# A priority for the activation chain of the first 24 units in a Fourier-and-feed-forward kernel

## The chip, the cores and the metric

The kernel runs on one core of a Trainium2 chip. The metric is device time in microseconds (us) for one execution of the whole program; the time before is 1764.74 us, the median of three runs.

## The reference, cut to what matters

```python
X = np.fft.fft(x, axis=1)            # x: (8, 3008, 256) float32
X = np.fft.fft(X, axis=2)
x = X.real.astype(np.float32).reshape(8 * 3008, 256)
h = x @ w_in                         # w_in: (256, 2048) float64
g = np.where(h >= 1, h, np.where(h <= -1, 0.0, (h + 1) ** 2 / 4))
out = (g @ w_out).astype(np.float32) # w_out: (2048, 256) float64
```

The inputs `w_in` and `w_out` are 64-bit floats that were drawn in numpy, so the kernel receives 64-bit words and has to make 32-bit floats of them.

## The kernel before, in words

The eight batches are worked off one after the other. Each has 3008 rows, which the kernel holds as three chunks of 482 to 512 columns (`NCHUNK`, `WIDTH`). The column direction is 2048 hidden features in 16 tiles of 128 (`NFT`). A **unit** is one chunk by one feature tile; each batch has 48 units (`per`), the whole kernel 384.

A unit has three parts. `gemm1` (L359) makes two products `uv` on TensorE in six matmuls; the weights `wh`/`wl` and the data `pqh`/`pql` are each split into a high and a low part. Then comes the **activation**, nine instructions on three engines: VectorE makes `us` (L362) and the two signs of `h` (L364, L365), ScalarE a ReLU and a square (L372, L373), VectorE the min/max (L374), ScalarE the rounded copy `gh` (L375), GpSimd the remainder `gl` in two halves (L378). Last, `gemm2` (L402) adds 12 matmuls with `woh`/`wol` into four accumulators. `gemm2` of a unit is given out `LAG` = 4 units after its `gemm1`. The buffers `uv` number 3, `us` 2, `h` and `a` 3, `gh` and `gl` 4.

The first batch is different. Its 48 units go in two visits: units 0 to 23 take feature tiles 0 to 7 of all three chunks, units 24 to 47 take tiles 8 to 15 and add to what the first visit stored. Meanwhile the weights are still being made. They come in 16 jobs of 512 columns; `convert_w(n)` (in short c0 to c15) turns a job's 64-bit words into 32-bit floats in six or seven VectorE instructions and one or two ScalarE ones (for c6 to c15: L208, L217, L218, L221, L222, L223, L224, L225). Jobs of `w_out` are then split into `woh`/`wol` (`split_w_out`, L169 on ScalarE and L170 on VectorE); jobs of `w_in` go through a small matmul and are split into `wh`/`wl` (`fold_w_in`, `fold_delta`). The `STEPS` table says in front of which unit each of these is given out:

```python
    0: "o2", 1: "f1 d1 o3 p11", 2: "p12", 3: "p13 p14 l8 l9", 4: "c6",
    5: "o6 c7", 6: "o7 l10", 9: "c8", 11: "c9 l11", 13: "f2 d2 c10 l12",
    15: "c11 l13", 17: "o10 c12 l14", 18: "o11", 19: "c13 l15", 20: "c14",
    21: "f3 d3", 22: "c15", 25: "o14", 26: "o15",
```

(`p11` to `p14` are the last pieces of the Fourier transform of batch 0, which also end in a split by L169 and L170.) Job 6 is what `gemm2` of feature tiles 4 and 5 needs (first in unit 4), job 7 tiles 6 and 7; jobs 8 and 9 are needed by `gemm1` of unit 24, jobs 12 and 13 by that of unit 28, jobs 14 and 15 by `gemm2` of units 28 and 30.

The order on each engine is written by the language's scheduler when the program is built. Each instruction gets a place number in the order in which the code gives it out; at each moment an engine takes, of the instructions whose inputs and buffers are ready by the scheduler's reckoning, the one with the lowest place. `tc.high_priority(offset=n)` lowers the place numbers inside it by n and puts the counter back when it ends. After that the order on an engine is fixed. The code already uses it for the copies out of the accumulators (`EVICT_AHEAD`).

Of the kernel before, what the change touches and what calls it, by code (L numbers as in the profile page):

```python
# [1 line left out]

# [1 line left out]

# [23 lines left out]
NFT = FF // P  # L28
LAG = 4
EVICT_AHEAD = 150  # L30

C_ORDER = [*range(1, 8), 0, *range(8, NC)]
WIDTH = [7 * NA + 34, CH, CH]
# [76 lines left out]
def fft_ffn_kernel(ctx: ExitStack, tc: tile.TileContext, x, cst, w_in, w_out, out):  # L110
# [223 lines left out]
    units = []  # L334
# [7 lines left out]
    per = NCHUNK * NFT  # L342
    n_units = len(units)
    acts, outs = {}, {}
# [5 lines left out]
    def gemm1(i):  # L350
        b, k, f, *_ = units[i]
        n = WIDTH[k]
        hi, lo = pq[b, k]
        cols = slice(f * P, (f + 1) * P)
        uv = []
        for m in range(2):
            t = ps.tile([P, CH], F32, tag="uv", name=f"uv_{i}_{m}", bufs=3)
            for j, (w, r) in enumerate(((wh, hi), (wl, hi), (wh, lo))):
                nc.tensor.matmul(t[:, :n], w[m][:, cols], r[:, m, :n], start=(j == 0), stop=(j == 2))  # L359
            uv.append(t[:, :n])  # L360
        us = sb.tile([P, CH], F32, tag="us", name=f"us_{i}", bufs=2)[:, :n]
        nc.vector.scalar_tensor_tensor(us, nyb[b, k][:, :n], delta[:, f : f + 1], uv[0], op0=ALU.mult, op1=ALU.add)  # L362
        h = sb.tile([P, 2, CH], F32, tag="h", name=f"h_{i}", bufs=3)[:, :, :n]
        nc.vector.tensor_tensor(h[:, 0], us, uv[1], op=ALU.subtract)  # L364
        nc.vector.tensor_tensor(h[:, 1], us, uv[1], op=ALU.add)  # L365
        a = sb.tile([P, 2, CH], F32, tag="a", name=f"a_{i}", bufs=3)[:, :, :n]
        gh = sb.tile([P, 2, CH], F32R, tag="gh", name=f"gh_{i}", bufs=4)[:, :, :n]
        gl = sb.tile([P, 2, CH], F32R, tag="gl", name=f"gl_{i}", bufs=4)[:, :, :n]


        for sl in (slice(0, 2),) if i < n_units - 1 else (slice(0, 1), slice(1, 2)):
            nc.scalar.activation(a[:, sl], h[:, sl], AF.Relu, bias=half, scale=0.5)  # L372
            nc.scalar.activation(a[:, sl], a[:, sl], AF.Square)  # L373
            nc.vector.scalar_tensor_tensor(h[:, sl], a[:, sl], 1.0, h[:, sl], op0=ALU.min, op1=ALU.max)  # L374
            nc.scalar.activation(gh[:, sl], h[:, sl], AF.Copy)  # L375
        for sg in range(2):
            eng = nc.vector if sg and i >= n_units - 3 else nc.gpsimd
            eng.tensor_tensor(gl[:, sg], h[:, sg], gh[:, sg].bitcast(F32), op=ALU.subtract)  # L378
        acts[i] = gh, gl

    accs = []
    def gemm2(i):
# [15 lines left out]
        for dh, sg in banks:  # L398
# [6 lines left out]
            if last:  # L405

                dst = o[dh][:, sg, :n]
                with tc.high_priority(offset=EVICT_AHEAD):
                    if v:
# [42 lines left out]
    for i in range(n_units + LAG):  # L452
        run_steps(STEPS.get(i, ""))
        if i < n_units:
            b, r = divmod(i, per)
# [11 lines left out]
            while pending and (change or not soon and done < total * (r + 1 - r0) / (per - r0)):  # L467
                change = False
                w, f = pending.pop(0)
# [61 lines left out]
```

## Time and profile before

| | |
|---|---|
| median of three runs | 1764.74 us (1764.58 to 1770.89) |
| profiled execution | 1765.38 us, of which the span from first to last instruction 1763.6 |
| busy in the span | TensorE 98%, VectorE 82%, ScalarE 76%, GpSimd 68% |
| granted TensorE clock, mean | 0.997 of full speed |

Times in the rows below are microseconds from the start of the span, durations in us unless a column says ns. PE is TensorE, PEld its weight loads, DVE VectorE, ACT ScalarE, POOL GpSimd, SP the engine that issues DMAs. A row of a timeline reads: start, duration, engine, line, operation, output and inputs with shapes, how many, and in brackets how long the engine sat idle before it and what ended that. L12 is line 12 of the kernel.

### The profile page before, as it was taken

To read this page: it belongs to the slowest core of one execution; us is meant where nothing else is said; L and a number is where in the kernel's file an instruction comes from. 1 tells how busy PE (TensorE), PEld (TensorE's weight loads), DVE (VectorE), ACT (ScalarE), POOL (GpSimd) and SP (SyncE) were. 2 spreads that over 40 slices of the span, in tenths; PEclk is the share of its full clock that TensorE was granted. 3 is DMA by queue.
4 is the path that set the end of the run, shared out by engine and by line. 5 is a ranking of instruction groups with operands and counts; after the bars stand their busy time and mean duration, and the time that the engine had idled before them with its cause. 6 is when DMAs were issued, how large, how long until landed. Compare 5 with 4: busy or idle time off the path is not lost.

```text
span 1763.6 us, 21942 instructions
## 1 busy us (share of the span) xinstructions
PE 1735.8 (98%) x7982; PEld 1420.5 (81%) x7982; DVE 1440.0 (82%) x1766; ACT 1346.3 (76%) x1580; POOL 1202.1 (68%) x838
## 2 busy tenths in 40 slices
PE   9988999999999999999999999999999999999998
PEld 6766888888888788888888888888888888888877
DVE  6999788888887888878888788878888788888887
ACT  5777877777777877777778877788778787777776
POOL 1545966776768766787667876677676766667775
PEclk9999999999999999999999999999999999999999
DMA  7013321010010100110001100011000000000000
GB/s 230 12 66 101 101 104 60 28 50 30 13 51 28 53 30 1 51 48 33 30 10 51 50 28 24 22 39 50 28 24 34 1 23 32 11 25 5 19 25 24
DMA packets 29963, 72.51 MB, mean 41 GB/s; under 512 B 2976, under 2 KB 8224, under 8 KB 29856
## 3 DMA queue, kind: packets, MB, share of 16 engines
q1 hardware_dynamic: 29568, 70.08, 12.1%
q8 instruction: 62, 1.02, 0.2%
q10 hardware_dynamic: 288, 1.05, 0.2%
q14 instruction: 45, 0.37, 0.1%
HBM read 43.31 MB, written 27.81 MB: 40 GB/s over the span
## 4 chain that ended last, share of the span: by engine, by line
PE 61%; ACT 10%; POOL 9%; issue 6%; DVE 5%; ACTq 0%; POOLq 0%; DVEq 0%
PE acc L402 38%; PE uv L359 19%; POOL gl L378 9%; DVE h L374 4%; ACT a L373 4%; ACT gh L375 3%; ACT a L372 3%; PE s L270 2%; PE s L309 2%; ACT z L280 1%; DVE o L414 0%; DVE h L365 0%; DVE h L364 0%; POOL y L131 0%; ACT o L412 0%
## 5 line engine op out<-in xcount | busy, mean ns | idle before, releaser
L378 POOL TENSOR_TENSOR gl<-h,gh 128x512 fp32r<-128x512 f32 (+1 forms) x765 | 1095.1, 1454 | 513.3 <-ACT gh L375 491.7
L374 DVE SCALAR_TENSOR_TENSOR h<-a,h 128x1024 f32<-128x1024 f32 (+1 forms) x385 | 578.0, 1502 | 219.7 <-ACT a L373 218.1
L375 ACT ACTIVATE gh<-h 128x1024 fp32r<-128x1024 f32 (+1 forms) x385 | 400.6, 1041 | 356.9 <-DVE h L374 344.2
L402 PE MATMUL acc<-gh,woh 128*128 128x512 f32 (+1 forms) x1536 | 608.3, 396 | 6.7 <-ACT gh L375 3.3
L402 PE MATMUL acc<-gl,woh 128*128 128x512 f32 (+1 forms) x1536 | 604.6, 394 | 9.1 <-POOL gl L378 9.1
L402 PE MATMUL acc<-gh,wol 128*128 128x512 f32 (+1 forms) x1536 | 596.2, 388 | 0.0
L372 ACT ACTIVATE a<-h,biases 128x1024 f32<-128x1024 f32 (+1 forms) x385 | 431.7, 1122 | 10.0 <-DVE h L365 7.7
L373 ACT ACTIVATE a<-a 128x1024 f32<-128x1024 f32 (+1 forms) x385 | 398.8, 1036 | 7.1
L402 PEld LDWEIGHTS acc<-gl,woh 128*128 128x128 f32 x1536 | 288.8, 188 | 76.4 <-POOL gl L378 16.8
L402 PEld LDWEIGHTS acc<-gh,woh 128*128 128x128 f32 x1536 | 289.3, 188 | 68.9 <-DVE o L414 5.5
L402 PEld LDWEIGHTS acc<-gh,wol 128*128 128x128 f32 x1536 | 289.5, 188 | 59.2
L364 DVE TENSOR_TENSOR h<-us,uv 128x512 f32<-128x512 f32 (+1 forms) x384 | 259.3, 675 | 67.2 <-POOL gl L378 27.3
L359 PE MATMUL uv<-pqh,wh 128*128 128x512 f32 (+1 forms) x768 | 303.7, 395 | 3.0 <-DVE us L362 2.9
L359 PE MATMUL uv<-pql,wh 128*128 128x512 f32 (+1 forms) x768 | 301.4, 392 | 0.0
L359 PE MATMUL uv<-pqh,wl 128*128 128x512 f32 (+1 forms) x768 | 299.5, 390 | 0.0
L362 DVE SCALAR_TENSOR_TENSOR us<-nyb,delta,uv 128x512 f32<-128x512 f32 (+1 forms) x384 | 278.5, 726 | 14.6 <-PE uv L359 13.8
L365 DVE TENSOR_TENSOR h<-us,uv 128x512 f32<-128x512 f32 (+1 forms) x384 | 256.0, 667 | 0.0
L359 PEld LDWEIGHTS uv<-pqh,wh 128*128 128x128 f32 x768 | 144.4, 188 | 40.9 <-DVE us L362 6.8
L359 PEld LDWEIGHTS uv<-pql,wh 128*128 128x128 f32 x768 | 144.6, 188 | 32.1
L359 PEld LDWEIGHTS uv<-pqh,wl 128*128 128x128 f32 x768 | 144.4, 188 | 30.5 <-issue 0.2
L131 POOL TENSOR_TENSOR y<-x 96x512 f32<-96x512 f32 x60 | 106.4, 1774 | 20.0 <-DMA x<-in_x_dram 8.2
L280 ACT ACTIVATE z<-s 64x192 f32<-64x192 f32 x256 | 86.6, 338 | 6.5 <-PE s L275 1.7
(54 smaller groups left out, 548.0 us busy)
## 6 DMA issues: line engine op xcount, KB each, us to landing
x<-in_x_dram SPq DMA_DIRECT2D x64, 384.0 KB, 3.3
out_dram<-o SPq DMA_DIRECT2D x30, 512.0 KB, 2.8
out_dram<-o SPq DMA_DIRECT2D x16, 482.0 KB, 3.0
nyb<-nyr SPq DMA_DIRECT2D x24, 256.0 KB, 3.4
raw<-in_moe_w_out_dram SPq DMA_DIRECT2D x8, 512.0 KB, 10.9
raw<-in_moe_w_in_dram SPq DMA_DIRECT2D x6, 512.0 KB, 4.5
part<-o SPq DMA_DIRECT2D x4, 512.0 KB, 3.2
o<-part SPq DMA_DIRECT2D x4, 512.0 KB
```

What stands on the lines that cost most here:

```text
L131: nc.gpsimd.tensor_tensor(y, t[:, 0], t[:, 1], op=ALU.add)
L280: nc.scalar.activation(dst, src, AF.Copy)
L359: nc.tensor.matmul(t[:, :n], w[m][:, cols], r[:, m, :n], start=(j == 0), stop=(j == 2))
L362: nc.vector.scalar_tensor_tensor(us, nyb[b, k][:, :n], delta[:, f : f + 1], uv[0], op0=ALU.mult, op1=ALU.add)
L364: nc.vector.tensor_tensor(h[:, 0], us, uv[1], op=ALU.subtract)
L365: nc.vector.tensor_tensor(h[:, 1], us, uv[1], op=ALU.add)
L372: nc.scalar.activation(a[:, sl], h[:, sl], AF.Relu, bias=half, scale=0.5)
L373: nc.scalar.activation(a[:, sl], a[:, sl], AF.Square)
L374: nc.vector.scalar_tensor_tensor(h[:, sl], a[:, sl], 1.0, h[:, sl], op0=ALU.min, op1=ALU.max)
L375: nc.scalar.activation(gh[:, sl], h[:, sl], AF.Copy)
L378: eng.tensor_tensor(gl[:, sg], h[:, sg], gh[:, sg].bitcast(F32), op=ALU.subtract)
L402: nc.tensor.matmul(acc[:, :n], w[:, f, wc], g[:, sg], start=(first and j == 0), stop=(last and j == 2))
```

## The change

The nine instructions of the activation move from `gemm1` into a function of their own, which `gemm1` calls at the same place. For units 0 to 23 (`per // 2` is 24) the call stands inside `tc.high_priority(offset=60)`; for all later units in an empty context. No instruction is added, removed or changed.

```diff
+AHEAD = 60
...
                 nc.tensor.matmul(t[:, :n], w[m][:, cols], r[:, m, :n], start=(j == 0), stop=(j == 2))
             uv.append(t[:, :n])
+
+        with tc.high_priority(offset=AHEAD) if i < per // 2 else nullcontext():
+            acts[i] = activate(i, uv)
+
+    def activate(i, uv):
+        b, k, f, *_ = units[i]
+        n = WIDTH[k]
         us = sb.tile([P, CH], F32, tag="us", name=f"us_{i}", bufs=2)[:, :n]
         nc.vector.scalar_tensor_tensor(us, nyb[b, k][:, :n], delta[:, f : f + 1], uv[0], op0=ALU.mult, op1=ALU.add)
...
             eng.tensor_tensor(gl[:, sg], h[:, sg], gh[:, sg].bitcast(F32), op=ALU.subtract)
-        acts[i] = gh, gl
+        return gh, gl
```

## Rows read from the trace of the kernel before

**Rows 1.** The page's first part: engines over the whole span.
```profile
PE 1735.8 (98%) x7982; PEld 1420.5 (81%) x7982; DVE 1440.0 (82%) x1766; ACT 1346.3 (76%) x1580; POOL 1202.1 (68%) x838
```

**Rows 2.** Busy time by stretch: window, its length, engines, granted clock, DMA.
```profile
37.00:170.00 133.00, 118.71 (x518) 89.81 (x517) 125.34 (x183) 96.89 (x115) 63.70 (x48) 0.99 0.17 54
170.00:260.00 90.00, 86.54 (x415) 70.69 (x414) 71.81 (x89) 70.96 (x97) 71.27 (x49) 1.00 0.31 98
260.00:500.00 240.00, 239.88 (x1125) 199.65 (x1124) 196.84 (x234) 185.66 (x216) 170.65 (x118) 1.00 0.12 39
```

**Rows 3.** TensorE's waits from 37 to 170: us in total, times, longest.
```profile
PE acc L402 <- POOL gl L378: 6.9, 13, 1.2
PE acc L402 <- ACT gh L375: 3.3, 3, 1.5
PE uv L359 <- DVE us L362: 2.9, 3, 1.3
PE s L309 <- DVE pql L170: 1.0, 1, 1.0
```

**Rows 4.** Timeline at 88 to 92.
```profile
88.21 0.42 DVE L217 TENSOR_SCALAR cv<-raw 128x512 uint32<-128x512 uint32 x1
88.54 0.42 DVE L221 TENSOR_SCALAR raw<-raw 128x512 uint32<-128x512 uint32 x1
88.88 0.68 DVE L218 SCALAR_TENSOR_TENSOR cv<-cv,cps 128x512 f32<-128x512 uint32 x1
...
90.61 0.74 DVE L362 SCALAR_TENSOR_TENSOR us<-nyb,delta,uv 128x512 f32<-128x512 f32 x1
...
91.41 0.50 PE L359 MATMUL uv<-pqh,wh 128*128 128x512 f32 x1 [1.35 <-DVE us L362]
```

**Rows 5.** VectorE's work by line, 37 to 170: busy us, mean ns, idle before.
```profile
L374 DVE SCALAR_TENSOR_TENSOR h<-a,h 128x1024 f32<-128x1024 f32 (+1 forms) x24 | 31.1, 1296 | 0.8 <-ACT a L373 0.5
L362 DVE SCALAR_TENSOR_TENSOR us<-nyb,delta,uv 128x512 f32<-128x512 f32 (+1 forms) x26 | 18.8, 727 | 5.0 <-PE uv L359 5.0
L364 DVE TENSOR_TENSOR h<-us,uv 128x512 f32<-128x512 f32 (+1 forms) x25 | 16.6, 666 | 0.0
L217 DVE TENSOR_SCALAR cv<-raw 128x512 uint32<-128x512 uint32 x10 | 7.3, 735 | 0.0
L224 DVE SCALAR_TENSOR_TENSOR cps<-raw,cps 128x512 uint32<-128x512 uint32 x10 | 6.9, 687 | 0.0
L223 DVE TENSOR_SCALAR cps<-raw 128x512 uint32<-128x512 f32 x10 | 6.8, 685 | 0.2 <-ACT raw L222 0.2
L225 DVE SCALAR_TENSOR_TENSOR cv<-cv,cps 128x512 f32<-128x512 f32 x10 | 6.8, 677 | 0.0
L218 DVE SCALAR_TENSOR_TENSOR cv<-cv,cps 128x512 f32<-128x512 uint32 x10 | 6.8, 676 | 0.0
L221 DVE TENSOR_SCALAR raw<-raw 128x512 uint32<-128x512 uint32 x10 | 5.3, 533 | 0.0
```

**Rows 6.** The same line L374 in the steady part, 260 to 1700.
```profile
L374 DVE SCALAR_TENSOR_TENSOR h<-a,h 128x1024 f32<-128x1024 f32 (+1 forms) x329 | 499.7, 1519 | 209.1 <-ACT a L373 207.9
```

**Rows 7.** TensorE's timeline at 130, and the stretch behind it.
```profile
130.28 0.50 PE L402 MATMUL acc<-gh,woh 128*128 128x512 f32 x1 [1.51 <-ACT gh L375]
132.00:135.00 3.00, 3.00 (x8) 2.35 (x8) 3.00 (x7) 2.22 (x3) 0.82 (x1) 0.50 0.85 287
```

**Rows 8.** Timeline: job 6 from its first VectorE step to its first use; job 7's last step and use.
```profile
51.53 0.42 DVE L217 TENSOR_SCALAR cv<-raw 128x512 uint32<-128x512 uint32 x1
62.76 0.69 DVE L170 TENSOR_TENSOR wol<-cv,woh 128x512 fp32r<-128x512 f32 x1
65.71 0.51 PE L402 MATMUL acc<-gh,woh 128*128 128x482 f32 x1
70.60 0.69 DVE L170 TENSOR_TENSOR wol<-cv,woh 128x512 fp32r<-128x512 f32 x1
78.35 0.38 PE L402 MATMUL acc<-gh,woh 128*128 128x482 f32 x1
```

**Rows 9.** Timeline of VectorE: the end of job 15's conversion.
```profile
162.67 0.68 DVE L225 SCALAR_TENSOR_TENSOR cv<-cv,cps 128x512 f32<-128x512 f32 x1
```

**Rows 10.** SP's waits over the whole span, as in rows 3; TensorE's waits from 165 to 260.
```profile
SPq L123 <- DVE cv L225: 9.6, 1, 9.6
SPq L189 <- DVE cv L225: 7.7, 1, 7.7
...
PE acc L402 <- POOL gl L378: 2.2, 3, 1.4
PE s L270 <- ACT z L280: 1.5, 2, 1.1
```

More of the change, by code (lines that the diff above doesn't have):

```diff
@@ L1 @@
-from contextlib import ExitStack
+from contextlib import ExitStack, nullcontext
 import numpy as np
```

## Prediction

> **What bounds the kernel now.** I read the page's engine shares first, then the busy time by stretch, then the waits and the work by line inside the stretch that the change touches. Over the whole span TensorE is busy 98% [rows 1], so the kernel can only get faster by the 2% in which it isn't. The stretches show where these are [rows 2]. From 260 to 500 us TensorE is idle for 240 − 239.88 = 0.1 us; there is nothing to win in the steady part. From 37 to 170 us, which is about where units 0 to 23 have their activations, it is idle for 133 − 118.71 = 14.3 us, and from 170 to 260 for 90 − 86.54 = 3.5 us. So the change plays for at most 14.3 us, or 0.8%, and a little that hangs on it.
>
> In the same stretch the other column to look at is VectorE: 125.34 of 133 us, 94%, against 71.81 of 90 right behind it and 82% later [rows 2]. It is VectorE that is full here, and TensorE's waits name it by its victims [rows 3]: 6.9 us for `gl`, 3.3 us for `gh`, 2.9 us for `us`, 1.0 us for a split of the transform. The first three, 13.1 us, are all ends or starts of an activation chain that came late. Why it came late is seen at 88 us [rows 4]: VectorE does three steps of a weight conversion from 88.21 on, takes `us` only at 90.61, and TensorE, which needs the bank that `us` empties, stands 1.35 us until 91.41. The conversion's weights aren't needed before unit 24.
>
> **The change part by part.** *Removed and added.* No instruction is added or taken away; the nine instructions of an activation are the same. Moving them into a function costs nothing on the chip.
>
> *Moved.* By the place numbers, an activation of units 0 to 23 goes 60 places forward. A unit's iteration takes six places for `gemm1` and twelve for `gemm2` (the nine of the activation use no places any more, since the counter is put back), and a conversion eight. From c6, given out in front of unit 4, to unit 4's activation it is 14 places, to unit 5's 42, to unit 6's 63. So an activation overtakes the conversions, splits and folds given out in front of its own unit and of the unit before, hardly those further back. That means each conversion falls back by about two units, not to the end: when VectorE has a choice, unit 6 comes behind c6 as before. No DMA is moved, and GpSimd runs nothing but `gl` until batch 1 is folded, given out from unit 25 on; ScalarE has room with 96.89 of 133 us [rows 2].
>
> *What it can give: VectorE's work is the bound.* Reordering doesn't shorten the 125.34 us. What can shrink is, first, VectorE's idle time in the stretch, 133 − 125.34 = 7.7 us, of which 5.0 us are waits of `us` for TensorE [rows 5]: moments in which the ready conversion steps had been used up early and no activation was ready. With activations in front, conversions are what is left to fill such holes. The bounds are 0 and 7.7; I take half of the 5.0, 2.5 us, because TensorE itself was busy in part of these holes and because a conversion also waits for ScalarE between its steps.
>
> *Second, work pushed out of the stretch.* One conversion costs VectorE (7.3 + 6.9 + 6.8 + 6.8 + 6.8 + 5.3) / 10 = 4.0 us [rows 5]. At its end c14 and c15 (given out in front of units 20 and 22) are done by 163.3 [rows 9], ahead of the min/max of units 22 and 23. Overtaken by two units each, both may fall behind them: between 0 and 8.0 us leave the stretch. But unit 24 is no longer raised, so it waits behind them, and its delay is covered only by the up to four units whose `gemm2` is still to do. VectorE has 18.2 idle us from 170 to 260 to take the work in [rows 2]. I take one of the two, 4.0 us.
>
> *Third, TensorE's clock.* After the longest of these idle times, 1.51 us at 128.8, the granted clock was 0.50 from 132 to 135 [rows 7], the lower level, 1.2 GHz: 3 us at half speed, 1.5 us lost. Whether that goes depends on what the idle times become; 0 to 1.5, I take 0.75.
>
> *What it can cost.* L374 takes 1296 ns on average in the stretch and 1519 in the steady part [rows 5, 6], where activations follow one another without conversions between them. If the first 24 units come to look like the steady part, that is 24 × 0.223 = 5.4 us more VectorE work just where VectorE is full. The bounds are 0 and 5.4; I take the middle, 2.7. The Trainium skill (SBUF — State Buffer, Who interferes with whom) speaks against the change here: a VectorE instruction with two SBUF inputs contends with a GpSimd one that reads SBUF, and the loser blocks for the whole instruction. L374 reads `a` and `h` from SBUF and L378 reads `h` and `gh`. By that rule the middle would rather be the full 5.4 and the sum below 1.9; the gap of the two rows agrees with its sign.
>
> *The weights' due times.* The first that could come late are those of job 6: `wol` is done at 62.76 + 0.69 = 63.45 and first used about 65.71, a slack of 2.3 us; job 7's, 70.60 + 0.69 = 71.29 against 78.35, 7.1 us [rows 8]. Two units of VectorE work are 2 × (0.727 + 0.666 + 0.666 + 1.296) = 6.7 us [rows 5]. So job 6 may keep TensorE waiting for 6.7 − 2.3 = 4.4 us, job 7 not. Bounds 0 and 4.4. I take 0: while TensorE waits for it, VectorE runs conversions that it would have had to run anyway, and it is VectorE's total that sets the end of the stretch. Jobs 8 to 15 are due from unit 24 on and are not tight.
>
> *SP's queue.* Loads of later weights and of batch 1 wait for buffers that a conversion's last step frees (9.6 and 7.7 us already), and they will move with it; but from 165 to 260 TensorE waits for nothing that a load brings [rows 10]. I take 0.
>
> Sum: −2.5 − 4.0 − 0.75 + 2.7 = −4.6 us. The profiled execution took 1765.38, so 1760.8; that execution lies 0.64 above the median, so the median after is 1760.1.
>
> **The rivals.** *A larger gain.* All of VectorE's holes are filled and both conversions leave the stretch: −7.7 − 8.0 + 2.7 = −13.0, which TensorE's 14.3 idle us just allow: 1751.7. For it speaks that 13.1 us of TensorE's waits are for activations; against it that VectorE is 94% busy already and would have to reach 100%.
>
> *Who waits is exchanged.* The conversions that fall back come due later in the stretch at the expense of other units; VectorE's holes and the work done by 170 us stay as they are: 1764.7. For it speaks that the overtaking is limited to two units.
>
> *Contention eats it.* The full 5.4 us and no gain: 1770.1. For it speaks the steady row of L374; against it that the conversions have steps of their own that get stretched (L217 735 ns on average, L221 533, the undisturbed ones 420 [rows 4, 5]), so that the change may trade one for the other.
>
> *Weights late* (slower). If three units overtake job 6's and job 7's chains, which alternate between VectorE and ScalarE and can lose their turn at every step, 10.1 us of delay leave waits of 10.1 − 2.3 = 7.8 and 10.1 − 7.1 = 3.0 us, 10.8 together, in which VectorE can't run ahead because the four `gh` and `gl` buffers are full: 1775.5. It decides once these waits pass 8.8 us plus what is gained elsewhere. Against it: job 7's slack, and that only parts of the chains are within 60 places of the third unit.
>
> **How the numbers follow.** About 0.5%, 8.8 us, is what a measurement of this kernel can tell from no change. I give the forecast (1756 to 1764) 0.42, the larger gain 0.20, the exchange 0.20, contention 0.08, late weights 0.10. Faster by over 0.5% means under 1755.9: the larger gain and the edge of the forecast, 0.22. Slower by over 0.5% means over 1773.6: late weights, 0.10. The rest, 0.68, is within. For the range I leave out the better half of the larger gain and most of the late weights: 1752 to 1770.
>
> **What would show it.** In the profile after, TensorE's idle time up to where unit 23's `gh` is made should fall from 14.3 to about 9 us, and its waits for `gl`, `gh` and `us` with it; VectorE should be over 94% busy up to there; c15's last step should stand behind the L374 of unit 23; VectorE should have less idle time in the 90 us behind; L374's mean should lie between 1296 and 1519 ns. `us` should follow its matmuls at once, unlike at 90.61. The prediction is wrong if TensorE waits for `woh` or `wol` by several us at unit 4 or 6, if its idle time moves to units 24 to 34 in full, or if the steady part, which I hold unchanged, moves by more than 2 us.

## The result, and the profile after

| | kernel before | kernel after |
|---|---|---|
| time, us: median (lowest to highest) | 1765.51 (1764.22 to 1770.89), 7 runs | 1772.08 (1771.12 to 1773.04), 7 runs |
| ratio to before, 95% interval | | 1.0032 [1.0021, 1.0043] |
| profiled execution, us; span | 1765.38; 1763.6 | 1772.56; 1770.8 |

The change made the kernel slower, by 0.3%, some 6 us. That is less than the 0.5% that the prediction takes as no change, but it goes the other way than the forecast of 1760.1, and it lies above the range of 1752 to 1770.

The page's first part for the kernel after, to hold against [rows 1]:

```profile
PE 1736.7 (98%) x7982; PEld 1420.9 (80%) x7982; DVE 1443.6 (82%) x1766; ACT 1348.5 (76%) x1580; POOL 1202.0 (68%) x838
```

Same instructions, and 3.6 us more VectorE time for them. The busy time by stretch of the kernel after; the first stretch is drawn 6 us longer than in [rows 2], since its work ends later:

```profile
37.00:176.00 139.00, 121.32 (x512) 90.20 (x511) 127.29 (x180) 97.62 (x115) 64.40 (x49) 0.96 0.16 52
176.00:260.00 84.00, 79.06 (x388) 64.98 (x387) 69.38 (x84) 68.45 (x95) 66.13 (x47) 1.00 0.34 106
260.00:500.00 240.00, 240.00 (x1126) 199.90 (x1125) 197.11 (x239) 185.52 (x214) 170.44 (x118) 1.00 0.12 39
```

From 260 us on nothing changed. In front of that TensorE is idle for 17.7 + 4.9 us, and VectorE, which was to be fuller than 94%, is at 127.29 / 139 = 92%. TensorE's waits from 37 to 176 of the kernel after, against [rows 3]:

```profile
PE uv L360 <- DVE h L373: 7.3, 5, 3.6
PE acc L410 <- POOL gl L386: 5.2, 10, 1.0
PE acc L410 <- ACT gh L383: 4.0, 3, 2.4
PE wps L247 <- DVE cv L226: 1.0, 1, 1.0
PE uv L360 <- DVE us L370: 0.2, 1, 0.2
```

The waits for `us` are all but gone and those for `gl` fell from 6.9 to 5.2 us, as forecast; those for `gh` rose from 3.3 to 4.0. New are 7.3 us for `h`, in few and long stops. The longest one, with what lies around it, in the kernel after's timeline:

```profile
72.17 0.64 ACT L209 ACTIVATE cps<-raw 128x512 f32<-128x512 uint32 x1
72.75 0.50 PE L360 MATMUL uv<-pqh,wh 128*128 128x512 f32 x1 [1.40 <-DVE h L373]
78.02 0.80 PE L360 MATMUL uv<-pqh,wh 128*128 128x512 f32 x1 [3.61 <-DVE h L373]
80.15 0.61 ACT L170 ACTIVATE woh<-cv 128x512 fp32r<-128x512 f32 x1
80.81 1.57 PE L410 MATMUL acc<-gh,woh 128*128 128x482 f32 x3
```

Before, job 6's turn on the `fft` bank and its `woh` came here:

```profile
52.51 0.62 ACT L208 ACTIVATE cps<-raw 128x512 f32<-128x512 uint32 x1
61.44 0.61 ACT L169 ACTIVATE woh<-cv 128x512 fp32r<-128x512 f32 x1
```

So job 6 is late. Its conversion gets its turn on the bank at 72.17 (52.51 before), behind four splits of the transform that use the same bank and had each lost their turn to raised activations. `woh` begins at 80.15, 18.7 us later than before (61.44), and unit 4's `gemm2` at 80.81 instead of 65.71 [rows 8]; in front of it TensorE stands 1.40 and 3.61 us. The trace puts these two stops down to `h` (L373), which empties a bank that `gemm1` needs; unit 4's second product, which could have filled them, had no `woh` yet. The prediction calls itself wrong "if TensorE waits for `woh` or `wol` by several us at unit 4 or 6", and in this sense the sign is there. Whether the late weights also cost the time is another question; the experiments give no sign of it.

VectorE's lines from 37 to 176 of the kernel after (busy us, mean ns, idle before), against [rows 5]:

```profile
L382 DVE SCALAR_TENSOR_TENSOR h<-a,h 128x1024 f32<-128x1024 f32 (+1 forms) x24 | 30.6, 1279 | 1.0 <-ACT a L381 1.0
L370 DVE SCALAR_TENSOR_TENSOR us<-nyb,delta,uv 128x512 f32<-128x512 f32 (+1 forms) x25 | 18.2, 729 | 3.8 <-PE uv L360 3.8
L372 DVE TENSOR_TENSOR h<-us,uv 128x512 f32<-128x512 f32 (+1 forms) x24 | 16.0, 668 | 3.4 <-POOL gl L386 3.4
```

VectorE waits 3.8 instead of 5.0 us for TensorE, and 3.4 us, in three stops, for something that cost it nothing up to 170 us before [rows 5] (from 170 to 176 it did once, 2.4 us): L372 writes `h`, and one of the three `h` buffers comes free only when GpSimd has made `gl` from it. The first of VectorE's waits, and the last step of job 15, in the timeline of the kernel after:

```profile
40.76 0.72 DVE L370 SCALAR_TENSOR_TENSOR us<-nyb,delta,uv 128x482 f32<-128x482 f32 x1 [1.99 <-PE uv L360]
50.32 0.66 DVE L372 TENSOR_TENSOR h<-us,uv 128x482 f32<-128x482 f32 x1 [1.07 <-POOL gl L386]
52.67 0.66 DVE L372 TENSOR_TENSOR h<-us,uv 128x482 f32<-128x482 f32 x1 [1.13 <-POOL gl L386]
177.84 0.68 DVE L226 SCALAR_TENSOR_TENSOR cv<-cv,cps 128x512 f32<-128x512 f32 x1
```

Job 15's conversion ends at 178.5 (163.3 before [rows 9]), behind the min/max of unit 23, which begins at 174.4: that much was pushed out of the stretch, as forecast.

How much of the loss is VectorE's? Unit 35's min/max, by which all conversions are done, ends at 228.3 before and at 236.0 after. VectorE from 20 us to there, first the kernel before, then after:

```profile
20.00:228.30 208.30, 190.40 (x877) 149.03 (x877) 183.10 (x265) 156.98 (x215) 114.92 (x84) 0.98 0.28 91
```

```profile
20.00:236.00 216.00, 193.18 (x884) 149.86 (x883) 189.02 (x266) 158.17 (x214) 114.73 (x84) 0.97 0.27 90
```

Of the 7.7 us, 5.9 are VectorE being busy longer (3.6 over the whole span), with 266 instructions for 265, and 1.8 are VectorE idle longer. That is bookkeeping, not yet a cause; but it names the two things to be tried, instructions that take longer and time stood still.

### The profile page after: what moved, and what is told of

Same layout as the page of the kernel before. It is cut to its first block, busy times and chain, and to the rows that moved or that the text cites. A ratio compares the mean times of both kernels' runs of the same rounds, so it can differ in the third digit from the quotient of the medians.

```text
span 1770.8 us, 21944 instructions
## 1 busy us (share of the span) xinstructions
PE 1736.7 (98%) x7982; PEld 1420.9 (80%) x7982; DVE 1443.6 (82%) x1766; ACT 1348.5 (76%) x1580; POOL 1202.0 (68%) x838
## 4 chain that ended last, share of the span: by engine, by line
PE 80%; POOL 3%; ACT 3%; issue 2%; DVE 2%; ACTq 0%; POOLq 0%
PE acc L410 50%; PE uv L360 25%; POOL gl L386 3%; PE s L271 2%; PE s L310 2%; DVE h L382 1%; ACT a L381 1%; ACT gh L383 1%; ACT a L380 0%; DVE o L422 0%; ACT z L281 0%; POOL y L132 0%; PE ny L288 0%; PE s L276 0%; DVE h L372 0%
## 5 line engine op out<-in xcount | busy, mean ns | idle before, releaser
L372 DVE TENSOR_TENSOR h<-us,uv 128x512 f32<-128x512 f32 (+1 forms) x384 | 259.4, 676 | 65.6 <-POOL gl L386 24.1
L373 DVE TENSOR_TENSOR h<-us,uv 128x512 f32<-128x512 f32 (+1 forms) x384 | 256.1, 667 | 0.0
## 6 DMA issues: line engine op xcount, KB each, us to landing
raw<-in_moe_w_out_dram SPq DMA_DIRECT2D x8, 512.0 KB, 11.6
```

## The experiments

All times are medians; the ratio is to the kernel before, run beside it. Beside the different runs the kernel before itself had medians of 1764.2 to 1768.3 us, so runs are best held against each other by their ratios.

| run | what it is | us | ratio [95% interval] |
|---|---|---|---|
| e1_early | raised: units 0 to 7 only | 1767.95 | 1.0020 [1.0011, 1.0029] |
| e2_late | raised: units 8 to 23 only | 1768.99 | 1.0023 [1.0014, 1.0032] |
| e3_mid | raised: units 8 to 13 only | 1767.36 | 1.0011 [1.0002, 1.0020] |
| e4_splits | after, the splits p11 to p14 raised too | 1777.58 | 1.0073 [1.0061, 1.0086] |
| e5_fold | after, folds f2 and f3 on the `fft` bank | 1772.21 | 1.0039 [1.0026, 1.0051] |
| e6_before_fold | before, with the same folds | 1767.51 | 1.0017 [1.0008, 1.0026] |
| e7_keep | e4 with eight conversions and splits raised too | 1770.38 | 1.0029 [1.0019, 1.0039] |
| e8_chain | before, with c8, c9, c12, c13 raised | 1766.38 | 1.0007 [0.9997, 1.0018] |
| e9_on | raised: units 0 to 47 | 1774.79 | 1.0057 [1.0044, 1.0069] |
| e10_half | raised by 30 places, not 60 | 1771.81 | 1.0039 [1.0026, 1.0051] |
| e11_fill | after, TensorE kept working in the stops | 1774.64 | 1.0054 [1.0040, 1.0068] |
| e12_lead | after, p13 and p14 behind jobs 6 and 7 | 1775.46 | 1.0060 [1.0047, 1.0073] |
| g1_before_pool | before, six `wol` on GpSimd | 1768.74 | 1.0017 [1.0006, 1.0028] |
| g3_before_load | before, 5.5 us more VectorE work | 1771.06 | 1.0026 [1.0016, 1.0036] |
| g4_before_nogl | before, no `gl` | 1745.48 | 0.9881 [0.9868, 0.9893] |
| g5_after_nogl | after, no `gl` | 1749.72 | 0.9903 [0.9890, 0.9916] |
| g6_early_nogl | units 0 to 7 raised, no `gl` | 1749.68 | 0.9901 [0.9887, 0.9915] |
| g7_late_nogl | units 8 to 23 raised, no `gl` | 1749.70 | 0.9898 [0.9878, 0.9918] |

**Which units.** The condition of the `with` is the only edit:

```diff
-        with tc.high_priority(offset=AHEAD) if i < per // 2 else nullcontext():
+        with tc.high_priority(offset=AHEAD) if i < 8 else nullcontext():              # e1_early
+        with tc.high_priority(offset=AHEAD) if 8 <= i < per // 2 else nullcontext():  # e2_late
+        with tc.high_priority(offset=AHEAD) if 8 <= i < 14 else nullcontext():        # e3_mid
+        with tc.high_priority(offset=AHEAD) if i < per else nullcontext():            # e9_on
```

> Only units 0 to 7 are raised. Theory A (the loss is made at the start: the four splits of the transform pieces p11 to p14 and then the conversion of job 6 go one after the other through one accumulator bank, each loses its turns to the raised activations, so woh of job 6 is late and TensorE stands in front of unit 4's second product): woh of job 6 is again ready only near 80 us, TensorE again idles over 4 us between 71 and 78, and the time is 3 to 6 us above before, 1768.5 to 1771.5. Theory B (the loss is spread evenly over all raised units, as contention or more VectorE work would spread it): a third of 6.6, 1767.7. Theory C (the loss is made at the end of the visit, where c12 and c13 come late and the fold f3 holds the uv banks): no loss, 1765.5 or a little less.

> Only units 8 to 23 are raised. Theory A: the start is that of before, woh of job 6 ready near 62 us, and what the middle gains shows: 1760 to 1764. Theory B: two thirds of the loss, 1769.9. Theory C: the whole loss, and more, since the start loses nothing and the end is as late as in the changed kernel: 1767 to 1772.

> Only units 8 to 13 are raised: neither the start nor the end of the visit is touched. Theory A: a small gain like that of the run with units 8 to 23, 1761 to 1765. Theory B: a quarter of the loss, 1767.2. Theory C: a gain, 1761 to 1764, and clearly less than the run with units 8 to 23.

> The changed kernel with the activation raised in all 48 units of the first token block instead of 24. Hand-over theory: TensorE's extra idle time of 4.6 us from 165 to 260 us comes from conversions and splits that were put off and now stand in front of the unraised activations of units 24 and on. Then raising these too takes most of it away: 1768 to 1769.5. Rival: what was put off is needed by then (jobs 14 and 15 by unit 28, the next block's transform by unit 48), so that raising on makes it later still: 1773 to 1777, with waits for weights or for the transform's banks. If it is the start alone that counts: 1771.5 to 1772.5.

Each half costs by itself, about 3 and 4 us, and together they make up the whole loss; no half of the change is good, and units 8 to 13 alone cost some 2 us. Of the three theories only B, an even spread, came near in all three runs (1767.7, 1769.9 and 1767.2 expected; 1767.95, 1768.99 and 1767.36 measured); A failed at e2_late and e3_mid, and C at e1_early and e3_mid. The sections below show that B was right in the sizes and only in part in its reason: the two halves lose in different ways. Raising on through unit 47 is no cure: the kernel gets slower still, as the rival had it, so nothing speaks for the hand-over at unit 24 as what loses the time.

**The late weights of job 6.** Two ways to bring them earlier with the activations still raised: the splits in front raised as well, or the two splits that unit 16 first needs moved behind jobs 6 and 7; then the conversions raised too, and as a counterpart the kernel before with four of them raised.

```diff
+        with tc.high_priority(offset=AHEAD) if b == 0 and h >= 2 else nullcontext():  # e4_splits, in stage2
-        split(hi, lo, pt.rearrange("p i (e d) -> p i e d", e=2))
+            split(hi, lo, pt.rearrange("p i (e d) -> p i e d", e=2))
-    3: "p13 p14 l8 l9",                                                               # e12_lead
+    3: "l8 l9",
-    6: "o7 l10",
+    6: "o7 p13 p14 l10",
+KEEP = "c6 o6 c7 o7 c8 c9 c12 c13".split()       # e7_keep, on top of e4_splits; e8_chain: before, "c8 c9 c12 c13"
+            with tc.high_priority(offset=AHEAD) if s in KEEP else nullcontext():
-            steps[s[0]](int(s[1:]))
+                steps[s[0]](int(s[1:]))
```

> The changed kernel (units 0 to 23 raised), in which the splits of the transform pieces p11 to p14, four instructions on ScalarE and four on VectorE, are raised by the same 60 places, so that they keep their place against the activations. Theory A: the bank is passed on early, woh of job 6 is ready before 68 us, TensorE's idle 5 us between 71 and 78 and the half clock behind it go, and the time falls by 4 to 7 us from 1772.1, to 1765 to 1768. Theory B: 2.7 us of VectorE work change places, no change, 1771 to 1773. Theory C: the end is as before this edit, 1771 to 1773.

> The changed kernel with the last two splits of the transform (p13, p14, whose data are first wanted in unit 16) moved from step 3 to step 6, behind the conversions of jobs 6 and 7, so that two links less stand in front of job 6's turn on the bank. Start theory: job 6's first half is there at 70 to 73 us instead of 80.2, the stops in front of unit 4 go from 5.0 to under 2.5 us, the granted clock of 75 to 100 us is over 0.93, and the time is 1767.5 to 1770. Rival: what comes earlier here is taken from weights that are wanted later (as with the splits raised), unit 24 is still 4 us or more behind the kernel before, and the time is 1771 to 1773 or more.

> The kernel of the run in which the transform's splits are raised too, with the conversions of jobs 6, 7, 8, 9, 12 and 13 and the splits of jobs 6 and 7 raised by the same 60 places as well: only c10, c11, c14 and c15, which have time, are still overtaken. Theory C: c9 ends before 97 us in place of 108.9 and c13 before 150 in place of 158.5, the first product of unit 13 starts before 105, and the time falls from 1777.6 to 1763 to 1767. Theory B: VectorE's work is the same, the time stays near 1777. A third reading (the loss is the hand-over at unit 24, which isn't raised and waits for c14 and c15): c15 stays late, and some 5 us of the loss stay, 1771.

> The kernel before, no activation raised, with c8, c9, c12 and c13 raised by 60 places: the opposite of the change. Theory C: the folds are ready earlier, units 13 and 21 start earlier, TensorE idles less: 1759 to 1764. Theory B and the forecast's own reasoning (activations late because of conversions): slower, 1766 to 1770.

The timelines of e4_splits and of e12_lead, job 6's `woh`:

```profile
72.97 0.63 ACT L170 ACTIVATE woh<-cv 128x512 fp32r<-128x512 f32 x1 [0.42 <-DVE cv L226]
```

```profile
72.78 0.61 ACT L170 ACTIVATE woh<-cv 128x512 fp32r<-128x512 f32 x1
```

Both did what they were made for: `woh` came 7.2 and 7.4 us earlier than at 80.15. In e12_lead unit 10's last product then began 6.5 us earlier than in the changed kernel (99.3 against 105.8), but unit 13's no earlier (126.3 against 125.6), and the time of both kernels went up, in e4_splits above what any theory expected, in e12_lead as the rival had it. So the chain through the one bank is why job 6 is late, but bringing job 6 forward won nothing. What made these two kernels slower than the changed one was not followed up. e7_keep, which gives the conversions their places back under the raised activations, is 7 us better than e4_splits and still behind the kernel before. Its time is the one that the hand-over reading expected (1771), but e9_on speaks against that reading. e8_chain moved nothing that can be measured.

**The clock behind the stops.** Behind the 3.61 us stop the granted clock is 0.52 from 78 to 84 us, so mostly at the lower level of 1.2 GHz. In e11_fill TensorE adds zero times a weight to the accumulator instead of standing still; two offsets make up for the places that the products take, and the order on the other engines changes by a few instructions.

```diff
+    zero = woh[:, NFT - 1, :P]
+    nc.scalar.activation(zero, cs[:, :P], AF.Copy, scale=0.0)
...
-        with tc.high_priority(offset=AHEAD) if i < per // 2 else nullcontext():
+        with tc.high_priority(offset=AHEAD + {9: 6, 10: 20}.get(i, 0)) if i < per // 2 else nullcontext():
...
+    def fill(count):
+        for _ in range(count):
+            mm = nc.tensor.matmul(accs[0][:, : WIDTH[0]], zero, wh[0][:, : WIDTH[0]], start=False, stop=False)
+            tc.keep_in_program_order(mm)
...
+            if i == 9:
+                fill(6)
             gemm1(i)
+            if i == 9:
+                fill(14)
+                gemm2(4)
...
-        if i >= LAG:
+        if i >= LAG and i != 8:
```

> The changed kernel, with 20 products of zero weights (6 and 14) put on TensorE where it stands still while it waits in front of units 9 and 10, so that it keeps working from 71 to 78 us; the order of the weights and of VectorE's work stays nearly as it is. Clock theory: the 3.6 us stop costs more than itself, because TensorE comes out of it at 1.2 GHz and products then start 0.43 instead of 0.23 us apart. Then the granted clock of 75 to 100 us goes from 0.86 to 0.95 or more, and the time falls by 2.0 to 3.5 us, to 1768.6 to 1770.1. Rival: VectorE sets the pace behind the stop anyway, so that a faster TensorE only waits more often. Then the clock rises all the same, TensorE's idle time from 80 to 110 us grows by what the clock gave, and the time stays at 1771.4 to 1772.8.

Two stretches of the kernel after, then the same of e11_fill (TensorE is the first busy figure, the granted clock the third from the end):

```profile
75.00:100.00 25.00, 21.98 (x85) 17.46 (x86) 24.20 (x35) 18.58 (x22) 11.57 (x9) 0.86 0.11 40
78.00:110.00 32.00, 31.98 (x125) 24.36 (x126) 29.99 (x44) 22.80 (x27) 16.02 (x12) 0.91 0.14 48
```

```profile
75.00:100.00 25.00, 22.50 (x91) 16.34 (x90) 24.98 (x35) 16.95 (x22) 11.23 (x9) 1.00 0.14 45
78.00:110.00 32.00, 30.08 (x123) 21.78 (x121) 30.60 (x43) 22.46 (x27) 16.67 (x12) 1.00 0.15 48
```

The clock came back in full, and TensorE spent it waiting: idle for 1.9 us from 78 to 110 where it was idle for 0.02. Unit 23's last product begins at 187.8 against 187.4. That is the rival's picture, though the time is 2 us above the rival's range. In the profiled executions the lag behind the changed kernel is 1.0 us by unit 31 and grows to over 3 us only behind unit 96, in the steady part; it wasn't followed up.

**The folds.** e5_fold and e6_before_fold take the folds off the banks of `gemm1`:

```diff
-        if f4 < 2:
+        if f4 < 4:
             return fft_bank(0, name)
```

> The changed kernel, in which the folds f2 and f3 take the one spare accumulator bank of the transform in place of the three uv banks. Theory C (the conversions c8, c9 and c12, c13 come late, and the folds that need them stand in front of the first product of units 13 and 21 on the uv banks, so that TensorE uses up its second products and then starts with nothing prepared): the first product of unit 13 no longer waits for the end of c9 (107.3 us) and starts near 95, that of unit 21 before 155, and the time falls from 1772.1 to 1762 to 1767. Theory A (the late start): unit 4 still waits for woh near 80 us, 1769 to 1772. Theory B (VectorE's total is what counts): 1771 to 1773.

> The kernel before with the same change of banks for f2 and f3, as a control. Theory C: units 13 and 21 start earlier here too, but the conversions are earlier, so that less is to be had: 1760 to 1765. Theories A and B: no change, 1764 to 1767, or slower, since the folds now wait for each other and for the conversions on one bank.

Unit 13's first product came at 98.5 us instead of 111.7, and the time stayed where it was. In e5_fold unit 23's last product begins only 0.7 us later than in the kernel before, but unit 27's 7.1 us later: the loss was moved. The banks are not the cause either, and the control got slower and not faster.

Five mends (e4_splits, e12_lead, e7_keep, e11_fill, e5_fold), and none brought the time back. That would fit if something is short for the whole stretch, and the next runs put a price on VectorE.

**VectorE's price.** One step, done twice for eight jobs:

```diff
         nc.vector.scalar_tensor_tensor(shifted, high, 0x80000000, shifted, op0=ALU.bitwise_and, op1=ALU.bitwise_or)
+        if 6 <= n < 14:
+            nc.vector.scalar_tensor_tensor(shifted, high, 0x80000000, shifted, op0=ALU.bitwise_and, op1=ALU.bitwise_or)
```

> The kernel before, with one step of the conversion (the one that puts the sign back, 685 ns, which gives the same value when done again) done twice for jobs 6 to 13: 8 x 0.685 = 5.5 us more work for VectorE between 50 and 155 us, nothing else. VectorE theory: from 37 to 176 us VectorE's time is the time, so that what it does longer or stands still longer moves the end one for one: 1768.5 to 1770.5. Rival: its work is not the measure, but which weights and banks come in which order: then up to half of it is taken up by the 5.0 us that it waits for TensorE there, and the time is 1765 to 1767.5.

5.5 us of work cost 4.6 us by the ratio (0.0026 × 1766) and 5.0 by the medians, 0.8 to 0.9 for one; the interval of the ratio, 2.8 to 6.4 us, leaves room for 0.5 to 1.2. VectorE from 20 us to the end of unit 35's min/max says the same:

```profile
20.00:233.60 213.60, 192.63 (x876) 147.23 (x875) 188.67 (x273) 157.44 (x215) 114.47 (x84) 0.98 0.28 88
```

It is busy 5.6 us longer than in the kernel before (183.10) and idle for 24.9 us instead of 25.2. So there is little slack on VectorE, in the order that the kernel had before too.

The other way, six subtractions off VectorE:

```diff
-    def split(hi, lo, src):
+    def split(hi, lo, src, engine=None):
...
-        nc.vector.tensor_tensor(lo, src, hi.bitcast(F32), op=ALU.subtract)
+        (engine or nc.vector).tensor_tensor(lo, src, hi.bitcast(F32), op=ALU.subtract)
...
-            split(*(t[:, fs].rearrange("p f e -> p (f e)") for t in (woh, wol)), f32s.pop(n))
+            split(*(t[:, fs].rearrange("p f e -> p (f e)") for t in (woh, wol)), f32s.pop(n), nc.gpsimd if n >= 6 else None)
```

> The kernel before, with the last subtraction of the second weight matrix for jobs 6, 7, 10, 11, 14 and 15 on GpSimd instead of VectorE: 6 instructions of some 0.85 us less for VectorE, 5.1 us. VectorE theory: 1760 to 1763, if GpSimd, busy half of the time, takes them without delaying the second operand of the products (it takes about 1.4 us for such a one). Rival (GpSimd's own delay and the contention with VectorE give it back): 1764 to 1767.

No gain, and slower by 3 us (1.1 to 4.9 by the interval; the single executions spread from 1766.0 to 1773.1): GpSimd took 1408 ns for each, and the time that VectorE was spared came back. In the profiled execution the min/max took 1455 ns on average from 37 to 236 us (1376 before), the conversions' exponent step (L221) 677 (533), and VectorE was idle for 14.7 us from 37 to 176 (10.1). What GpSimd does is not free for VectorE, so this run puts no price on VectorE's work alone.

**Without GpSimd.** The low part of the activation is left out; the third product takes zeros. (In both kernels the loads that borrowed the `gl` buffers at the start keep three buffers of that name.)

```diff
-        gl = sb.tile([P, 2, CH], F32R, tag="gl", name=f"gl_{i}", bufs=4)[:, :, :n]
+        gl = none[:, :, :n]
...
-        for sg in range(2):
-            eng = nc.vector if sg and i >= n_units - 3 else nc.gpsimd
-            eng.tensor_tensor(gl[:, sg], h[:, sg], gh[:, sg].bitcast(F32), op=ALU.subtract)
```

> The kernel before without the low part of the activation: GpSimd subtracts nothing, and the third product of each group takes a tile of zeros; the output lacks that correction. TensorE's work is the same. It is the counterpart of the same cut in the changed kernel and shows how much of the start is set by GpSimd: its waits (4.5 us or so of TensorE's) and VectorE's longer instructions beside it are gone, so 1750 to 1762, and VectorE's min/max takes 0.9 to 1.2 us instead of 1.3 in the stretch from 37 to 176 us.

> The changed kernel without the low part of the activation, as in the counterpart. Contention theory: the changed order lost because VectorE's instructions met GpSimd's more often (the conversions' first mask 0.32 us longer each, the min/max of units 24 to 35 0.19 us longer) and because a unit's buffers came free only with GpSimd's subtraction, on which VectorE now stands still for 2.2 us at 50 us. Then without GpSimd the difference between the two falls from 6.6 us to 2 or less. Order theory: the weights of jobs 6 to 9 come later whatever GpSimd does, since the activations stand in front of them; then the difference stays at 5 us or more.

The pair differs by 4.2 us instead of 6.6, and the four executions of each don't overlap (1744.02 to 1748.13, 1749.58 to 1749.86). So some 4 us of the loss need no GpSimd, and neither theory as it was put is right: the expectation was 2 or less, or 5 or more. The counterpart itself came out below its range (1745.48 against 1750 to 1762), and its min/max at 1.25 us, not under 1.2. VectorE in the pair, first g4_before_nogl, then g5_after_nogl:

```profile
37.00:75.00 38.00, 33.51 (x169) 27.79 (x169) 36.87 (x58) 30.00 (x37) 0.00 (x0) 1.00 0.01 2
20.00:176.00 156.00, 143.90 (x662) 113.53 (x662) 142.54 (x224) 118.78 (x161) 6.91 (x7) 0.97 0.26 84
```

```profile
37.00:75.00 38.00, 30.67 (x146) 24.61 (x146) 33.63 (x51) 28.42 (x34) 0.00 (x0) 0.96 0.02 7
20.00:176.00 156.00, 141.39 (x649) 111.19 (x648) 137.82 (x215) 114.83 (x153) 6.98 (x6) 0.96 0.24 79
```

With raised activations VectorE gets 4.7 us less done by 176 us (137.82 against 142.54), and the spans differ by 4.7 us (1747.7 and 1743.0). Of these, 3.2 us are lost before 75 us, where it stands still for 4.4 instead of 1.1 us. With GpSimd at work VectorE stands still for 1.4 and 4.4 us in the same stretch; first the kernel before, then after:

```profile
37.00:75.00 38.00, 32.59 (x160) 25.60 (x159) 36.63 (x57) 29.04 (x36) 16.02 (x12) 1.00 0.01 3
```

```profile
37.00:75.00 38.00, 31.68 (x151) 24.52 (x149) 33.60 (x49) 27.74 (x33) 17.07 (x14) 0.96 0.04 16
```

The other part is in the means of VectorE's lines from 37 to 236 us. The kernel before, then after, then g4_before_nogl's and g5_after_nogl's min/max:

```profile
L374 DVE SCALAR_TENSOR_TENSOR h<-a,h 128x1024 f32<-128x1024 f32 (+1 forms) x38 | 52.3, 1376 | 1.7 <-ACT a L373 1.4
L170 DVE TENSOR_TENSOR wol<-cv,woh 128x512 fp32r<-128x512 f32 x8 | 6.9, 864 | 0.0
```

```profile
L382 DVE SCALAR_TENSOR_TENSOR h<-a,h 128x1024 f32<-128x1024 f32 (+1 forms) x36 | 51.1, 1421 | 4.0 <-ACT a L381 3.9
L218 DVE TENSOR_SCALAR cv<-raw 128x512 uint32<-128x512 uint32 x10 | 9.2, 935 | 0.0
L171 DVE TENSOR_TENSOR wol<-cv,woh 128x512 fp32r<-128x512 f32 x8 | 7.3, 910 | 0.0
L222 DVE TENSOR_SCALAR raw<-raw 128x512 uint32<-128x512 uint32 x10 | 5.8, 584 | 0.0
```

```profile
L378 DVE SCALAR_TENSOR_TENSOR h<-a,h 128x1024 f32<-128x1024 f32 (+1 forms) x40 | 50.1, 1253 | 5.4 <-ACT a L377 4.8
```

```profile
L386 DVE SCALAR_TENSOR_TENSOR h<-a,h 128x1024 f32<-128x1024 f32 (+1 forms) x39 | 49.0, 1259 | 7.3 <-ACT a L385 7.0
```

Without `gl` the order makes no difference to an instruction: 1253 and 1259 ns here, 423 and 421 for the conversions' first mask (L218 of the kernel after), 424 and 423 for the exponent (L222), 685 in both for `wol`. With `gl` the first three are longer in every order and `wol` in all but e1_early, and by how much depends on the order. Over the prices without `gl` (1256, 422, 424, 685 ns), for 36 min/max, 10 masks, 10 exponents and 8 `wol`, that makes

| | min/max | mask | exponent | `wol` | excess, us |
|---|---|---|---|---|---|
| before | 1376 | 735 | 533 | 864 | 4.3 + 3.1 + 1.1 + 1.4 = 9.9 |
| after | 1421 | 935 | 584 | 910 | 5.9 + 5.1 + 1.6 + 1.8 = 14.4 |
| e1_early | 1365 | 707 | 465 | 683 | 3.9 + 2.9 + 0.4 + 0 = 7.2 |
| e2_late | 1454 | 627 | 836 | 911 | 7.1 + 2.1 + 4.1 + 1.8 = 15.1 |
| e10_half | 1541 | 981 | 618 | 870 | 10.3 + 5.6 + 1.9 + 1.5 = 19.3 |

The table separates the two halves of the change: raising units 8 to 23 makes VectorE's instructions 5.2 us longer in sum, raising units 0 to 7 makes them 2.7 us shorter and must lose its 3 us in another way. The stretch from 20 us to the end of unit 35's min/max shows which, first e1_early, then e2_late:

```profile
20.00:232.00 212.00, 192.75 (x881) 150.58 (x880) 181.30 (x265) 158.43 (x215) 112.09 (x84) 0.96 0.28 89
```

```profile
20.00:233.80 213.80, 193.91 (x879) 150.42 (x878) 189.71 (x265) 156.67 (x214) 116.27 (x84) 0.96 0.27 88
```

Against the kernel before (busy 183.10, idle 25.2 us) e1_early is busy 1.8 us less and idle 5.5 us more, e2_late is busy 6.6 us more and idle 1.1 us less.

**Half the distance.** The one edit is `AHEAD = 30`.

> The changed kernel with the activation raised by 30 places instead of 60, so that it overtakes about the conversions of its own unit and no more. Start theory (one bank through which four splits and then job 6's conversion go one after another, each losing its turn to raised activations): fewer turns are lost, job 6's first half of the weights is there between 68 and 76 us instead of 80.2, the stops in front of unit 4 shrink from 5.0 us to 2 to 3, and the time is 1768 to 1770. Rival (any raising costs the same, since it is the sum of VectorE's work with more contention that counts): 1771 to 1773, and the weights about as late.

`woh` came at 68.5, and VectorE stands still for only 1.8 us from 37 to 75 us (36.23 busy). Yet the time is that of the changed kernel. By the table this order has the most contention of all, 9.4 us over before, and up to the end of unit 35's min/max it is all in the busy time:

```profile
20.00:236.90 216.90, 196.85 (x879) 152.24 (x879) 192.62 (x265) 158.12 (x216) 113.69 (x83) 0.95 0.26 84
```

That is 9.5 us busy longer and 0.9 us idle less than before. So the dose did not halve the loss; one part of it was exchanged for the other.

**The halves without GpSimd.** As g5_after_nogl, with the conditions of e1_early and e2_late.

> Without the low part of the activation, as the pair before it, with the activation of units 0 to 7 alone raised. Stand-still theory: in the first raised units VectorE waits in its own order for things that are not yet there (3.2 us more idle from 37 to 75 us than in the counterpart that raises nothing), whatever GpSimd does; the loss of the whole change that is left without GpSimd, 4.2 us, comes from here: 3 to 4.7 us above that counterpart, a ratio to the kernel before of 0.9899 to 0.9910. Rival (the loss comes from the later units): within 1.5 us of it, 0.9875 to 0.9890.

> Without the low part of the activation, with the activation of units 8 to 23 alone raised. With GpSimd at work this half of the change cost 4.0 us while VectorE's fixed set of instructions took 6.3 us longer and stood still no longer. Contention theory: without GpSimd that cost goes: within 1.5 us of the counterpart that raises nothing, a ratio of 0.9873 to 0.9890. Rival (the order of the weights and folds costs it): 3 us or more above it, 0.9898 or more.

g6_early_nogl is as slow as the whole change without `gl`, a ratio of 0.9901 against 0.9903. As far as these ratios can tell, what is left of the loss without GpSimd comes from units 0 to 7, and with these raised units 8 to 23 add nothing to it that can be measured. VectorE stands still for 4.4 us from 37 to 75 us in it as well (33.56 busy). g7_late_nogl is undecided: three of its six executions took 1745.2 to 1746.2 us, at most 0.8 us over the counterpart's median, and three 1753.2 to 1756.0 at a lower granted clock (0.991 to 0.993 against 0.998). Its interval holds both answers.

VectorE from 20 us to the end of unit 35's min/max in g4_before_nogl, g5_after_nogl, g6_early_nogl and g7_late_nogl (one of its three short executions):

```profile
20.00:218.90 198.90, 185.63 (x870) 148.63 (x870) 174.42 (x265) 155.77 (x213) 15.73 (x14) 0.97 0.29 93
```

```profile
20.00:223.60 203.60, 188.33 (x878) 150.38 (x878) 175.55 (x265) 156.97 (x214) 16.74 (x14) 0.97 0.28 92
```

```profile
20.00:223.90 203.90, 189.84 (x884) 150.57 (x883) 175.26 (x266) 157.05 (x215) 16.77 (x14) 0.97 0.29 95
```

```profile
20.00:220.40 200.40, 186.90 (x883) 148.55 (x883) 175.96 (x266) 156.21 (x215) 16.72 (x14) 0.99 0.29 96
```

Its idle time is 24.5, 28.0, 28.6 and 24.4 us. Raising units 0 to 7 makes VectorE stand still, with GpSimd and without; raising units 8 to 23 makes its instructions longer, by 6.6 us with GpSimd and 1.5 without.

No variant of the order beats the kernel before.

## Why the prediction was wrong

**The view of the kernel held.** VectorE is what is full up to 176 us, and g3_before_load prices a us of it at 0.8 to 0.9. The steady part stayed, and TensorE's waits from 37 to 176 us name no load.

**The step that failed is the first gain**: "With activations in front, conversions are what is left to fill such holes." It is the other way round. The order on VectorE is fixed when the program is built. In the kernel before, conversions stood in front of activations and were ready, and so VectorE worked while TensorE or GpSimd finished what the next activation needed. With the activations in front it reaches them too soon: at 38.8 it waits 1.99 us for unit 1's products, at 49.3 and 51.5 for a buffer that GpSimd still reads. Ready conversions stand behind. Here is one, the sign step of an early conversion, first in the kernel before; then in the kernel after, with the step that it needs:

```profile
37.10 0.69 DVE L224 SCALAR_TENSOR_TENSOR cv<-raw,cv 128x512 uint32<-128x512 uint32 x1
```

```profile
37.12 0.42 DVE L224 TENSOR_SCALAR cv<-cv 128x512 uint32<-128x512 f32 x1
44.29 0.69 DVE L225 SCALAR_TENSOR_TENSOR cv<-raw,cv 128x512 uint32<-128x512 uint32 x1
```

It could have run from 37.5 on, and stood behind the whole stop at 38.8. VectorE's idle time from 37 to 75 us went from 1.4 to 4.4 us, and over the whole stretch from 139 − 128.94 = 10.1 (before, 37 to 176) to 139 − 127.29 = 11.7, where the sum had −2.5. That this part exists without GpSimd and lies in units 0 to 7 is shown by the runs without `gl`, in which 3.5 of the 4.7 us up to unit 35 are idle time; that the standing still is its mechanism is read from the traces, and no run took it away by itself and nothing else. Nor does each us of it cost one: in e11_fill VectorE is idle for 6.6 us from 37 to 75, 2.2 more than in the kernel after, and unit 35's min/max ends only 0.9 us later.

The row from which the premise was read shows it in part only. Of the 2.4 us from 88.21 to the `us` at 90.61 [rows 4] the three conversion steps took 1.3; the rest was another activation, which raising does not overtake:

```profile
89.48 1.21 DVE L374 SCALAR_TENSOR_TENSOR h<-a,h 128x1024 f32<-128x1024 f32 x1
```

**The second gain, −4.0, was none.** The work left the stretch as forecast, with job 15 ending at 178.5 instead of 163.3. But a conversion that is done later is not a conversion less. Units 17 to 19 did finish 0.5 to 1.4 us ahead of before; with the postponed conversions to be done, unit 20 was 4.6 us behind and unit 23 5.9. The step counted as won what was only lent.

**The clock, −0.75.** The dip at 132 us went (granted clock 1.00 from 132 to 135), and others came at 51 us (0.67 from 51 to 54) and 78 us. In e11_fill the longest of them, at 78, was filled and up to unit 23 nothing was won: TensorE waits for VectorE there anyway. No run tests the dip at 132, but by the same reading the term should have been 0.

**Contention, +2.7 of 0 to 5.4,** had the right sign and was too small: +4.5 us by the table. It was looked for in one instruction only. The min/max of the raised units stayed at 1279 ns ([rows 5]: 1296); the conversions' masks, pushed into the time when GpSimd makes `gl`, went from 735 to 935, and the min/max got longer only from 176 us on. The Trainium skill (SBUF — State Buffer, Who interferes with whom) says that a VectorE instruction with two SBUF inputs contends with a GpSimd instruction that reads SBUF, and that a `tensor_scalar` can contend with GpSimd too, in a mode that uses both pairs of ports. The runs agree: min/max and `wol` (two SBUF inputs) and the masks and exponents (`tensor_scalar`, operands in SBUF) got shorter without `gl`, while after's L372, with one input in PSUM, took 668 ns with `gl` and 670 without, and the conversions' four steps with an operand in the `fft` bank 676 to 687 with and 682 to 691 without.

**Late weights, taken as 0.** The overtaking was misjudged ("hardly those further back"): job 6's chain lost its turn again and again and came 18.7 us late, not two units' 6.7. No run shows a price for it: e4_splits and e12_lead brought the weights 7 us earlier and e10_half 11.6, and none won time, though each changed other things with it. So the rival of late weights describes what one sees at unit 4, with 5.0 us of stops, and nothing shows it to be the cause.

In sum: −2.5 became a loss, −4.0 and −0.75 became 0, +2.7 became +4.5 less what VectorE's price takes off. The two parts measured apart, 4.2 us without GpSimd and 4.5 × 0.8 to 0.9 = 3.6 to 4.1 us of contention, come to some 8 and the loss is 6 to 6.6. So they are not independent; that an engine that stands still meets GpSimd less often would explain it and fits e1_early, but isn't shown. Why VectorE's other idle time up to unit 35, over 20 us, does not take in the 3 us lost at the start stays open, and so does the half from unit 8 on without GpSimd.

## What to carry to other kernels

Where an engine is full and its order is fixed, as VectorE's here, ready work without a deadline was worth more in front of work that may have to wait than behind it; "let the urgent go first" pays only if the urgent is ready. Put a price on the engine first, with some us of harmless extra work, before the visible stops are mended: here five mends at the places where TensorE stood still did not bring the time back. And count work that is moved out of a stretch as moved, not as saved.

## What the runs showed that was not expected

- GpSimd's subtraction costs the whole kernel 20 us (1745.48 against 1766.06), though GpSimd is busy for only 68% of the span [rows 1] and TensorE's own work is the same; without it TensorE is busy for all of the 1440 us from 260 to 1700.
- The same 128 x 512 mask takes 0.42 us on average in every order without `gl`, and 0.57 (e3_mid) to 0.98 us (e10_half) beside it, by the order alone.
- 20 products of zeros held the granted clock at 1.00 where the stop had brought it to 0.52, and the time did not fall.
